# Local and global attention with a three-way max-out layer on one core: another literal order for the first third of the program

## The chip, the cores and the metric

The kernel runs on one core of one Trainium2 chip. The metric is device time in microseconds (us): a lower number is better. Five engines take part: PE (matrix products; PEld is its weight load), DVE (vector), ACT (scalar and activation), POOL (GpSimd) and SP, which here only issues DMA transfers.

## The reference

Batch 8, 8 heads, 576 positions, 64 per head. Attention is computed twice and added: once on q, k, v averaged over groups of four positions (144 of them), once on all positions but only within a band of three to either side. The sum, seen as 4608 tokens of 512 numbers, goes through a layer of three products whose maximum is taken, and a last product.

```python
out_d = sm_attn(q_d, k_d, v_d)                  # pooled by 4: 144 positions
out_up = np.repeat(out_d, factor, axis=2)
mask = np.abs(pos[:, None] - pos[None, :]) < factor
scores = np.where(mask, scale * np.matmul(q, k.transpose(0, 1, 3, 2)), -1000000000.0)
...
x = (out_up + out_local) as (4608, 512)
h = np.maximum(np.maximum(x @ w1, x @ w2), x @ w3)   # 512 -> 768
out = h @ w_out                                       # 768 -> 512
```

## The kernel before

**Tiling.** The eight batches are eight blocks j of 576 tokens, each cut into two halves n = 2j and 2j + 1. A half's pooled attention has scores (`ps`), a maximum taken negative (`nm`), an exponential on ACT, a sum whose reciprocal is `rd`, the scaled weights `pd`, `pdt`, `ptail`, their transposes on PE (`pt`, `ptt`), and the product with the pooled values (`vd` and `vs`, made from `hv` and `th`). For the first two blocks (n = 0 to 3, the dense ones) the band is done with matrix products as well: scores into a bank, maximum `mxb`, exponential, sum `zb`, and a multiplication by the reciprocal, all in one large tile whose traced name is `prod` (program name `early`). Other blocks do the band on DVE, POOL and ACT with elementwise products (`prod`, `pv`, `sums`). The max-out layer splits its numbers into a high and a low part: `xhi`, `xlo` for the tokens (made from `t` = `x` + `od`, the sum of both attentions) and `whi`, `wlo` for the weights (made from bf16 pieces `hh`, `wo`, `pv` and an f16 piece `hqk`). Three products (hi*hi, hi*lo, lo*hi) of 128x512 are added in a PSUM bank `pm`; the second product is `pm<-wo_0r,hh_0r`.

**Buffers.** PSUM has four banks `pm`, three `pa` and one `pq`. An operation that opens a bank waits until all readers of its previous use are done.

**What sets the order.** Every operation is recorded first, with a number (0 to 5409), its needs and the engines that may do it. A literal list, `TABLE` (lines 79 to 267), is then read word by word by `follow`: `546P` is operation 546 on PE, `145-146A` two operations on ACT; D is DVE, G is POOL, S is SP. `3F` stands for three fill products on PE (128x448, bf16, from a zeroed `prod`) whose results nobody reads; `warm` makes them. Within an engine the list's order is the order of the instructions, and its letters decide the engine. `take` also keeps a clock of estimated times from `price`, and by it chooses among the free buffers. `emit` then issues all instructions from one line, so that every instruction of the trace bears L765 (L764 in the changed kernel, whose file is one line shorter).

**Places that the text below speaks of.** Operation 546 is the first big product of the layer (block 0, `pm<-xhi_0r,whi_0r`); it needs 293 and 296 (`t<-x,od`, the attention's sum) and their casts 294, 297 (`xhi_0r<-t`) on ACT. Operation 104 (128x384) and 103 (128x256) are the last two multiplications of the dense band by the reciprocals (`prod<-prod,zb`) of half 1; their results are transposed on PE. 243 is the pooled attention's last product of half 1 (`pa<-pt,vd`). 361 and 362 are the corresponding multiplications of half 2, transposed by 375 to 378; 586 (`hh_0r<-pm,hh_0r`) is the end of the first max-out, and 628 the first product that opens its bank again.

Of the kernel before, what the change touches and what calls it, by code (L numbers as in the profile page):

```python
# [88 lines left out]
273S 559-562P 548P 347P 587P 549P 573-574P 303A 281A 299D 300A 289D 267D 274D 301D 304D 349P 550P 575P 563-564P 576-577P 565P 551P 578P 566-567P 579P
552P 568-569P 553-557P 580-582P 570P 583P 271A 343D 272D 290D 311A 282D 275D 312D 558A 247A 291A 276A 571D 584D 585A 335S 414S 345S 344S 415G 277G  # L90
374G 350P 387P 588-591P 613P 592P 600-602P 593-594P 614-618P 603-606P 619P 595-598P 607-608P 355-356D 351-352D 357A 353A 358D 354D 359-362D 1F
375-378P 609-610P 320S 449S 450G 283S 321A 313A 586D 380P 611P 628P 305S 346S 330S 451S 315S 887-888S 284A 285D 286A 306D 322D 287G 325S 381D 379A
599A 292G 416G 612D 307D 316A 317D 326D 331A 388P 382-383P 366-367S 323A 308A 324D 365D 371D 641P 629P 654P 642P 655P 630P 620-622P 631-637P 643-644P
638P 623P 639P 318A 640A 389P 624P 669P 309G 452G 645-648P 670-671P 649P 372D 327D 336A 332D 314D 337D 453D 368D 625D 417S 896S 496S 369-370S 461S
521S 386S 516S 459-460D 672P 650-652P 656-659P 673P 390P 660P 674P 661-665P 675-680P 395-396D 391-392D 653D 328A 512A 385A 418G 329G 319G 889A 338A
339G 373G 397A 398D 393A 681A 333A 506S 526S 895S 464S 498S 394D 419D 399-400D 402D 401D 682-689P 695P 408P 403-406P 690-692P 696P 693P 409A 407A
410-411P 697-706P 666D 667A 626A 513D 507-508D 522D 517A 384A 523D 668D 518D 694D 527-528D 627D 413A 509A 514A 412A 515G 519A 723P 420-421P 423D 422D
424D 524A 425-426A 529A 427-428A 890D 520G 710P 724-725P 736P 726-728P 737P 729-730P 738-740P 510G 741P 731P 711P 742-743P 712-713P 732P 714-715P
744-745P 716-717P 746P 718-721P 733P 536S 530D 497D 429-430A 431-432D 436D 438D 707D 433A 708A 434A 437D 439D 709D 537A 499G 525G 500G 462-463G 722A
440P 747P 442P 734P 435D 538D 735D 764P 468P 441P 751P 531S 465G 897A 532A 443-445P 765P 792P 752-757P 541S 448A 447A 446A 454P 758-762P 766-768P 926S  # L100
903S 908S 904S 533D 542D 748D 543D 534A 544A 749A 891D 750D 898D 471D 457-458A 455-456A 467P 769-771P 777P 535G 778-781P 466G 909G 1019S 1006S 927G
910G 1020G 928G 1021G 872G 875G 334G 900S 916S 970S 917G 901G 763A 905A 469-470D 899D 782-784P 793-794P 812P 785P 772P 813P 795P 814P 773-774P 786P
815P 796-797P 787P 798P 775P 799-802P 816-820P 803P 821-822P 788P 472A 539A 473A 906D 960S 1007S 912S 911S 474-477A 478-479D 485D 484A 545D 480A 486D
873A 902G 540G 968G 918G 874G 929S 892S 1500S 930G 489-492P 804P 823P 483D 776D 481-482D 789D 852P 487-488P 853P 824-825P 495A 494A 493A 790A 805P
501P 826P 854P 907D 913A 791D 827P 1128P 806P 828P 807-809P 1129P 829P 876A 502A 505A 503-504A 914-915D 1008A 830A 810A 893-894G 1501G 881G 978G 878G
931G 932P 935D 933-934D 919D 1502D 920-921D 936D 879A 880D 882A 937A 922A 938-939A 1009D 1014S 1016A 940A 923-924D 1010D 1035S 1484S 1015S 811S 1022S
1048S 831S 1485G 883G 1049G 925G 976G 877G 1017D 1030S 1508S 1023S 1036G 965G 1037G 972G 974G 1050G 1509G 1045S 1027S 966G 1510G 967G 1028G 855P
832-833P 1125P 856-857P 834-839P 858P 840-845P 859-866P 846P 1126P 1130P 1134P 847-849P 867P 1127P 1131P 868-869P 961A 850A 1018D 1166P 1132-1133P
1137-1139P 1143-1145P 870A 1151P 1135-1136P 1140-1142P 1146P 1152P 1147-1148P 1153P 1024A 975A 1025D 1149A 941A 942-943D 971A 1032A 945A 963-964A
1179P 1167-1168P 1154-1158P 1150D 1026D 1192P 1159-1162P 1169-1171P 1180P 1193-1194P 1172-1173P 1195P 1181P 1174P 1196-1199P 1175P 1200-1201P  # L110
1176-1177P 1202P 1182-1184P 1203P 1163D 948D 977G 1029G 973G 1164A 962A 1031S 1033D 990S 1479-1480S 1011S 950A 1178A 1481A 1165D 1220-1222P 1207P
1223P 1208P 1185-1188P 1209P 1189-1190P 1046G 979G 992A 995A 944A 991G 993G 1486G 994G 953P 1210P 1224-1226P 954-955P 1227-1228P 1211-1212P 1229P
1213-1217P 1034D 1038-1039D 1040G 1041A 1521S 1218P 980S 1230P 1614S 1487S 969D 1047G 1012G 988G 1013G 998G 996A 984A 982A 997A 851S 1089S 1488S 1606S
985G 981G 1000G 1522G 999G 1615G 947D 1482D 949D 986A 1191D 1204D 951P 946D 1483D 1042D 952P 956P 1219A 958A 1233-1237P 959D 1205A 957A 987A 983A
1206D 1274P 1231P 1232D 1043D 1044G 1238-1242P 1001P 1261-1262P 1243-1244P 1275P 1489A 1002A 1004-1005A 1003A 1248-1250P 1051P 1276-1278P 1251-1254P
1263P 1255-1256P 1279-1280P 1264-1265P 1257-1259P 1266-1269P 989D 1490D 1245D 1491D 1523G 1607G 1097G 1079S 1492S 1495S 1503S 1496S 1090A 1093G 1091A
1080A 1246A 1247D 1053D 1497A 1095A 1260A 1054D 1052D 1498D 1289P 1302P 1290-1292P 1303P 1293-1294P 1304P 1270-1271P 1295P 1272P 1296-1299P 1273D
1300P 1281P 1315P 1305P 1316P 1282-1283P 1317P 1284P 1499D 1081A 1085A 1055-1056A 1083A 1505A 1057A 1301A 1330P 1285P 1058-1060A 1061-1062D 1286D
1331-1332P 1306-1308P 1318P 1309P 1319-1321P 1333-1334P 1322P 1310-1311P 1335-1336P 1312-1313P 1323-1326P 1086G 1608G 1087G 1493-1494G 1096G 1084G
1094G 1082G 1598S 1518S 1599G 1519G 1092G 1098G 1520G 1632S 1633G 1616G 1504S 1099S 1609S 1109S 2042S 1103A 1287A 1506D 1288D 1067D 1064A 1069D 1066D  # L120
# [311 lines left out]
class Recorder:  # L432
# [104 lines left out]
    def price(self, eng, method, args, kw):  # L537

        out = kw["out"] if "out" in kw else args[0]
        n = elems(out)  # L540
# [4 lines left out]
        if eng == "PE":  # L545
# [3 lines left out]
            if args[1].dtype == F32R:  # L549
                return 226.7, False  # L550
# [1211 lines left out]
```

## Time and profile before

| | |
|---|---|
| device time, median of 3 runs | 684.52 us (684.20 to 684.93) |
| the profiled execution | 684.14 us; span of its trace 682.3 us |
| mean granted clock of PE | 0.999 |
| PE busy | 673.0 us, 99% |
| DVE / ACT / POOL busy | 616.1 / 403.5 / 392.9 us (90% / 59% / 58%) |

The span is the stretch from the first to the last instruction; 1.84 us of the profiled time lie around it. Busy times are sums over an engine's instructions; the share is of the span.

### The profile page before, as it was taken

How to read it: one execution, taken by the hardware profiler on the slowest of the kernel's cores; microseconds unless marked ns; L12 is line 12 of the kernel's file. 1: busy time of each engine (PE TensorE's matmuls, PEld its weight loads, DVE VectorE, ACT ScalarE, POOL GpSimd, SP SyncE). 2: the span in 40 equal slices, each digit the busy share in tenths (PEclk: the TensorE clock that was granted, in tenths of full speed). 3: DMA queues.
4: the chain of work that ended last, by engine and by line, in shares of the span. 5: the costliest groups of instructions: out<-in, count | busy, mean ns of one | idle time of the engine just before them, and what ended most of it. 6: DMA issues, size and time to landing. Idle time of an engine off the chain costs nothing.

```text
span 682.3 us, 12571 instructions
## 1 busy us (share of the span) xinstructions
PE 673.0 (99%) x4279; PEld 541.4 (79%) x4279; DVE 616.1 (90%) x846; ACT 403.5 (59%) x1366; POOL 392.9 (58%) x602
## 2 busy tenths in 40 slices
PE   7999999999999999999999999999999999999997
PEld 4678777878787788778877887788878888888886
DVE  7998999998999999999999999999998898999620
ACT  5955665788668457838675766457675654434121
POOL 3336377999989675939684977558356313332000
PEclk9999999999999999999999999999999999999999
DMA  9887475645455654435464535333430010000012
GB/s 317 298 294 264 166 224 174 202 153 182 145 180 164 207 182 155 152 126 175 146 190 138 160 124 159 106 107 97 144 97 19 1 61 1 1 0 1 0 62 62
DMA packets 50178, 92.79 MB, mean 136 GB/s; under 512 B 5540, under 2 KB 19426, under 8 KB 50114
## 3 DMA queue, kind: packets, MB, share of 16 engines
q1 hardware_dynamic: 50114, 91.99, 41.8%
q8 instruction: 33, 0.54, 0.3%
q14 instruction: 31, 0.25, 0.1%
HBM read 82.53 MB, written 9.44 MB: 135 GB/s over the span
## 4 chain that ended last, share of the span: by engine, by line
PE 96%; DVE 2%; DMA 1%; SPq 0%; issue 0%; ACT 0%; DVEq 0%
PE pm L765 80%; PE pa L765 14%; PE pq L765 2%; DMA whi<-in_kt_dense_dram 1%; DVE prod L765 1%; DVE zb L765 0%; DVE nm L765 0%; SPq L765 0%; DVE mxb L765 0%; DVE hh L765 0%; DVE t L765 0%; DVE wo L765 0%; DVE hqk L765 0%; DVE x L765 0%; DVE pd L765 0%
## 5 line engine op out<-in xcount | busy, mean ns | idle before, releaser
L765 PE MATMUL pm<-xhi_0r,wlo_0r 128*128 128x512 f32 x540 | 209.2, 393 | 0.0
L765 PE MATMUL pm<-xhi_0r,whi_0r 128*128 128x512 f32 x540 | 208.9, 394 | 0.0
L765 PE MATMUL pm<-xlo_0r,whi_0r 128*128 128x512 f32 x540 | 208.8, 394 | 0.0
L765 ACT ACTIVATE pv<-v,sums 128x64 f32<-128x64 f32 x564 | 148.5, 410 | 27.7 <-DVE x L765 12.1
L765 POOL TENSOR_TENSOR pv<-v,sums 128x256 f32<-128x256 f32 x237 | 143.0, 701 | 7.9 <-DVE x L765 5.8
L765 PE MATMUL pm<-wo_0r,hh_0r 128*128 128x512 f32 x576 | 142.1, 394 | 0.0
L765 PEld LDWEIGHTS pm<-wo_0r,hh_0r 128*128 128x128 f32 x576 | 106.4, 188 | 22.1 <-issue 0.7
L765 PEld LDWEIGHTS pm<-xlo_0r,whi_0r 128*128 128x128 f32 x540 | 101.4, 188 | 22.0 <-issue 1.6
L765 PEld LDWEIGHTS pm<-xhi_0r,whi_0r 128*128 128x128 f32 x540 | 101.4, 188 | 21.2 <-issue 1.2
L765 PEld LDWEIGHTS pm<-xhi_0r,wlo_0r 128*128 128x128 f32 x540 | 101.5, 188 | 21.1 <-issue 0.4
L765 DVE TENSOR_TENSOR prod<-k,pq 128x1792 f32<-128x1792 f32 x56 | 112.5, 2008 | 0.5
L765 DVE TENSOR_REDUCE sums<-prod 128x28 f32<-128x1792 f32 x56 | 112.1, 2002 | 0.3
L765 DVE TENSOR_REDUCE x<-pv 128x256 f32<-128x1792 f32 x40 | 79.8, 2009 | 0.8 <-POOL pv L765 0.8
L765 ACT COPY y<-pm 128x512 f32<-128x512 f32 (+1 forms) x50 | 28.7, 580 | 46.6 <-PE pm L765 38.4
L765 POOL TENSOR_TENSOR pv<-pv 128x768 f32<-128x768 f32 (+1 forms) x32 | 49.6, 1550 | 2.7 <-ACT pv L765 1.0
L765 POOL TENSOR_TENSOR x<-whi_0r,wlo_0r 128x512 f32<-128x512 f32 x16 | 22.9, 1445 | 47.4 <-DVE x L765 32.3
L765 ACT CAST hh_0r<-pm 128x512 fp32r<-128x512 f32 x47 | 27.6, 590 | 35.6 <-DVE pm L765 35.5
L765 ACT COPY t<-pm 128x512 f32<-128x512 f32 x42 | 24.6, 587 | 18.1 <-PE pm L765 17.7
L765 DVE TENSOR_TENSOR t<-pm,t 128x512 f32<-128x512 f32 x43 | 29.4, 684 | 6.0 <-PE pm L765 5.6
L765 ACT COPY pq<-q 128x256 f32<-128x256 f32 x56 | 22.2, 396 | 20.6 <-DVE prod L765 18.9
L765 DVE TENSOR_TENSOR pm<-pm,t 128x512 f32<-128x512 f32 x44 | 30.5, 693 | 4.1 <-PE pm L765 3.5
L765 DVE TENSOR_TENSOR hh_0r<-pm,hh_0r 128x512 fp32r<-128x512 f32 x47 | 32.1, 684 | 1.6 <-ACT hh_0r L765 1.4
(383 smaller groups left out, 1045.9 us busy)
## 6 DMA issues: line engine op xcount, KB each, us to landing
k<-in_k_dram SPq DMA_DIRECT2D x55, 320.0 KB
v<-in_v_dram SPq DMA_DIRECT2D x54, 320.0 KB
out_dram<-y SPq DMA_DIRECT2D x35, 256.0 KB
q<-in_q_dram SPq DMA_DIRECT2D x56, 128.0 KB
hqk<-in_kt_pool_dram SPq DMA_DIRECT2D x24, 256.0 KB
hqk<-in_qt_pool_dram SPq DMA_DIRECT2D x24, 256.0 KB
wo<-in_w_in_dram SPq DMA_DIRECT2D x8, 511.8 KB
hh<-in_w_in_dram SPq DMA_DIRECT2D x6, 511.8 KB
```

The costliest lines, as they stand in the source:

```text
L765: getattr(self.engines[o.eng], method)(*map(real, args), **{k: real(x) for k, x in kw.items()})
```

## The change

The list is another one from its 89th entry to about its 1980th of some 5443; the first 88 entries and the last 3463 are the same. As an engine sees it, the first 18 operations of PE, 29 of DVE, 23 of ACT, 6 of POOL and 23 of SP are unchanged, and so are the last 1980, 505, 464, 342 and 173. 122 operations go to another engine (DVE has 846 operations before and 856 now, ACT 795 and 799, POOL 563 and 549); there are 33 fills before and 32 now. The other edit is in `price`: the estimate for a big product is written as a formula, (512 + 32) / 2.4 = 226.7, which is the constant that stood there. The diff, with the list cut to one line of each:

```diff
 TABLE = """
 6S 11D 8D 2D 4D 18D 3D 9S 5D 0-1D 10S 340D 884-885D 7A 13-14S 126S 12S 129S 24-25P 167S 44P 21D 45P 169S 22D 1F 26P 19-20S 62D 42S 46P 27D 16S 127G
...
-188P 572P 348P 231P 229P 232-233P 547P 295G 230P 234P 187A 189A 1F 190P 269A 236-237A 235A 182A 266A 243P 245-246A 244A 191D 270D 262D 279A 302D 280D
...
             if args[1].dtype == F32R:
-                return 226.7, False
+                return (n + 32) / 2.4, False
```

What stands where now is seen in the order of the engines' instructions. On DVE, around the last multiplications of the dense band of half 1 (`prod<-prod,zb` with `zb_252`), before:

```order
L765 TENSOR_SCALAR zb_252<-zb_252 128x10
L765 TENSOR_TENSOR vs_538<-th_217 128x64
L765 RECIPROCAL zb_252<-zb_252 128x10
L765 TENSOR_TENSOR t_541<-x_376,od_461 128x512
L765 TENSOR_TENSOR hv_242<-v_168 128x256
L765 TENSOR_TENSOR t_544<-x_483,od_461 128x512
L765 TENSOR_TENSOR prod_119<-prod_119,zb_252 128x384
L765 TENSOR_TENSOR prod_119<-prod_119,zb_252 128x256
L765 TENSOR_SCALAR rd_335<-pa_238 128x5
```

and now, at the same place:

```order
L764 TENSOR_SCALAR zb_252<-zb_252 128x10
L764 RECIPROCAL zb_252<-zb_252 128x10
L764 TENSOR_TENSOR prod_119<-prod_119,zb_252 128x256
L764 TENSOR_TENSOR vd_514<-hv_242 128x256
L764 TENSOR_TENSOR prod_119<-prod_119,zb_252 128x384
L764 TENSOR_TENSOR t_517<-x_472,od_480 128x512
L764 TENSOR_TENSOR t_519<-x_386,od_480 128x512
L764 TENSOR_SCALAR rd_328<-pa_171 128x5
```

The two sums `t<-x,od` and the preparations `vs` and `hv` stood ahead of the two multiplications and are now behind them or gone from this engine; `vd`, which POOL made, is now on DVE between the two.

On PE, around the first big product (`xhi_0r,whi_0r`), a fill being a weight load and a 128x448 product of `prod_119`, before:

```order
L765 MATMUL pm_166<-prod_119 128x448
L765 MATMUL pq_431<-y_329,pv_257 64x58 x16
L765 MATMUL pq_431<-prod_119,pv_257 64x48 x2
L765 MATMUL pm_162<-ident_152,prod_119 128x128 x4
L765 MATMUL pm_156<-xhi_0r,whi_0r 128x512
L765 MATMUL pm_158<-ident_152,prod_119 128x128
L765 MATMUL pm_166<-xhi_0r,whi_0r 128x512
L765 LDWEIGHTS prod_119
L765 MATMUL pa_171<-prod_119 128x320
L765 MATMUL pa_230<-ident_152,pd_340 128x128
L765 MATMUL pa_238<-ident_152,pdt_343 128x128
```

and now:

```order
L764 MATMUL pm_156<-ident_152,prod_119 128x128
L764 LDWEIGHTS prod_119
L764 MATMUL pm_162<-prod_119 128x448
L764 MATMUL pm_166<-ident_152,prod_119 128x128
L764 MATMUL pq_451<-y_322,pv_257 64x58 x16
L764 MATMUL pq_451<-prod_119,pv_257 64x48 x2
L764 LDWEIGHTS prod_119
L764 MATMUL pm_158<-prod_119 128x448
L764 LDWEIGHTS prod_119
L764 MATMUL pm_162<-prod_119 128x448
L764 MATMUL pm_156<-ident_152,prod_119 128x128
L764 MATMUL pm_158<-xhi_0r,whi_0r 128x512
```

Before, the four transposes of operations 183 to 186 follow the band's products with `pv_257` in one run, and the fifth (188) comes behind the first big product. Now 183, 184 and 185 come earlier with fills between them (the row at the top is 185), then a fill, 188, the band's products, two fills and 186, and all five stand ahead of the first big product.

On PE, at the pooled weights of half 2 (`pdt`, `pd`, `ptail` transposed with `ident_152`), in the trace of before some 57 us behind the first big product, before:

```order
L765 MATMUL pm_162<-xhi_0r,wlo_0r 128x512
L765 MATMUL pa_171<-ident_152,pdt_343 128x128
L765 MATMUL pm_156<-xlo_0r,whi_0r 128x512
L765 MATMUL pa_238<-ident_152,pd_340 128x128
L765 MATMUL pm_162<-xlo_0r,whi_0r 128x512
L765 MATMUL pm_166<-xhi_0r,whi_0r 128x512
L765 MATMUL pa_230<-qkT_288 32x144 x4
L765 MATMUL pa_171<-ident_152,ptail_0_125 128x128
L765 MATMUL pm_158<-xhi_0r,whi_0r 128x512
L765 MATMUL pa_238<-ident_152,pd_340 128x128 x3
L765 MATMUL pm_166<-xhi_0r,wlo_0r 128x512
```

and now:

```order
L764 MATMUL pm_162<-xlo_0r,whi_0r 128x512
L764 MATMUL pm_156<-xlo_0r,whi_0r 128x512
L764 MATMUL pa_238<-ident_152,pd_368 128x128
L764 MATMUL pa_171<-ident_152,pdt_332 128x128
L764 MATMUL pa_171<-ident_152,ptail_0_125 128x128
L764 MATMUL pa_238<-ident_152,pd_368 128x128 x3
L764 MATMUL pm_162<-xhi_0r,whi_0r 128x512
```

The six transposes stood in four places between big products, and are now one run. Over the whole changed stretch the runs of transposes that have a big product on either side become fewer in this way: 28 before, 15 now.

## Rows read from the trace of the kernel before

**Rows 1.** The page: busy time by engine, and the chain that ended last.

```profile
PE 673.0 (99%) x4279; PEld 541.4 (79%) x4279; DVE 616.1 (90%) x846; ACT 403.5 (59%) x1366; POOL 392.9 (58%) x602
...
PE 96%; DVE 2%; DMA 1%; SPq 0%; issue 0%; ACT 0%; DVEq 0%
```

**Rows 2.** Waits of PE over the whole span: us in total, times, longest.

```profile
PE pm L765 <- DMA prod<-in_band_dram: 3.3, 1, 3.3
PE pm L765 <- DMA whi<-in_kt_dense_dram: 1.4, 2, 1.2
PE pm L765 <- DVE prod L765: 0.7, 3, 0.3
```

**Rows 3.** Busy time by stretch (start:end, length, engines, clock, DMA share, GB/s).

```profile
12.00:31.00 19.00, 18.28 (x272) 12.15 (x269) 18.39 (x55) 16.84 (x84) 7.04 (x11) 1.00 0.92 342
31.00:52.00 21.00, 21.00 (x293) 16.21 (x292) 20.54 (x42) 13.71 (x30) 5.79 (x6) 1.00 0.80 280
52.00:232.00 180.00, 180.00 (x1385) 143.11 (x1384) 168.17 (x221) 121.63 (x414) 146.88 (x216) 1.00 0.58 188
```

**Rows 4.** Timeline of PE around the first big product (start, us, instruction).

```profile
25.42 1.12 PE L765 MATMUL pm<-prod 128*128 128x448 bf16 x5
...
30.65 0.48 PE L765 MATMUL pm<-xhi_0r,whi_0r 128*128 128x512 f32 x1
...
33.94 0.71 PE L765 MATMUL pa<-pt,vd 128*64 128x144 f32 x8
```

**Rows 5.** Timeline of DVE, the multiplications of the dense band of half 1.

```profile
26.14 0.89 DVE L765 TENSOR_TENSOR prod<-prod,zb 128x256 f32<-128x256 f32 x2
...
27.29 0.63 DVE L765 TENSOR_TENSOR t<-x,od 128x512 f32<-128x512 f32 x1
27.83 0.42 DVE L765 TENSOR_TENSOR hv<-v 128x256 f32<-128x256 f32 x1
28.17 0.68 DVE L765 TENSOR_TENSOR t<-x,od 128x512 f32<-128x512 f32 x1
28.77 1.42 DVE L765 TENSOR_TENSOR prod<-prod,zb 128x384 f32<-128x384 f32 x2
```

**Rows 6.** Timeline of POOL and of ACT there, and the page's group of small ACT products.

```profile
28.33 1.11 POOL L765 TENSOR_TENSOR vd<-hv 128x256 f32<-128x256 f32 x1 [4.58 <-DVE hv L765]
...
29.00 0.14 ACT L765 ACTIVATION_READ_ACCUMULATOR pa<-pa,nm 128x1 f32 x1
29.05 1.14 ACT L765 CAST xhi_0r<-t 128x512 fp32r<-128x512 f32 x2
...
L765 ACT ACTIVATE pv<-v,sums 128x64 f32<-128x64 f32 x564 | 148.5, 410 | 27.7 <-DVE x L765 12.1
```

**Rows 7.** Timeline of PE: five transposes in one run, then two taken apart.

```profile
71.57 0.39 PE L765 MATMUL pm<-xhi_0r,whi_0r 128*128 128x512 f32 x1
71.80 0.71 PE L765 MATMUL pa<-ident,prod 128*128 128x128 f32 x5
72.26 0.48 PE L765 MATMUL pm<-xlo_0r,whi_0r 128*128 128x512 f32 x1
72.58 0.39 PE L765 MATMUL pm<-xhi_0r,whi_0r 128*128 128x512 f32 x1
...
87.45 0.39 PE L765 MATMUL pm<-xhi_0r,wlo_0r 128*128 128x512 f32 x1
87.68 0.27 PE L765 MATMUL pa<-ident,pdt 128*128 128x128 f32 x1
87.70 0.48 PE L765 MATMUL pm<-xlo_0r,whi_0r 128*128 128x512 f32 x1
88.02 0.27 PE L765 MATMUL pa<-ident,pd 128*128 128x128 f32 x1
...
88.36 0.40 PE L765 MATMUL pm<-xhi_0r,whi_0r 128*128 128x512 f32 x1
```

**Rows 8.** Timeline of DVE and of PE near 50 us, half 2's multiplications and transposes.

```profile
49.12 0.90 DVE L765 TENSOR_TENSOR prod<-prod,zb 128x256 f32<-128x256 f32 x2
49.93 0.69 DVE L765 TENSOR_TENSOR hh_0r<-pm,hh_0r 128x512 fp32r<-128x512 f32 x1
...
51.54 0.60 PE L765 MATMUL pa<-ident,prod 128*128 128x128 f32 x4
```

More of the change, by code (lines that the diff above doesn't have):

```diff
@@ L89 @@
[L89 to L120, printed above, removed]
@@ new lines @@
+1094A 1273D 1274P 1300P 1093A 1056-1059A 1498-1499D 1518S 1503S 1505A 1301A 1333-1341P 1342A 1090A 1302P 1085-1086G 1082G 1080G 1083G 1523G 1084G
+1081G 1088G 1593S 1508S 1509G 1614S 1095G 1510G 1519G 1097G 1504S 1099S 1275-1279P 1060A 1506D 1109S 1098G 1303P 1280P 1343P 1281P 1344-1345P
+1282-1285P 1061-1062D 1066D 1068D 1507D 1286D 1511D 1069D 1595A 1067A 1106A 1315P 1304-1312P 1316-1323P 1313P 1314D 1064D 1458-1459P 1346P 1324-1326P
+1100A 1104A 1287A 1288D 1347P 1072-1074P 1460-1461P 1348P 1356-1357P 1107G 1116G 1112G 1117G 1101G 1115G 1111G 1103A 1110A 1113A 1327D 1512D
@@ new lines @@
+1472P 1465P 1604D 1389A 1554A 1568-1569A 1611A 1605D 1455D 1567A 1456A 1473-1474P 1466P 1475P 1398P 1414-1417P 1432P 1399P 1418-1420P 1433-1436P
+1421-1423P 1476D 1561D 1612D 1400-1401P 1467-1468P 1424-1427P 1457D 1469D 1402-1403P 1428P 1429A 1617S 1619A 1477A 1437P 1711P 1404-1405P 1712P 1406P
+1438-1439P 1714P 1407P 1715-1716P 1720P 1408P 1618S 1390S 1636G 1560G 1565G 1570G 1563G 1600G 1637G 2058S 1632S 2042S 1582S 1616G 1564G 1571G 1572S
+1613D 1478D 1585A 1470A 1471D 1409A 1587A 1589G 1588G 1586G 1584G 1573G 2043G 1575G 1590G 1633G 1574G 1576A 1583A 1579A 1620-1621D 1625-1627D
@@ new lines @@
+1440-1443P 1713P 1444-1447P 1717P 1752P 1448P 1753-1755P 2046S 2037S 1410S 2045S 2066S 2076S 2038S 1680S 1580G 1592G 1718P 1756P 1524P 1721P 1449A
+1577A 1719P 1723P 1757-1759P 1765-1767P 1724P 1768P 1722P 1769P 1760P 1725P 1578A 1628A 1527D 1526D 1629D 1525D 1528D 1761P 1729-1731P 1735A
+1762-1763P 1529-1530A 2039A 1531-1532A 1764A 1533A 1581D 1630D 1591D 1726-1728P 1737-1738P 1732-1733P 1739P 1734P 1770-1776P 1736D 1777D 1740-1744P
+1806-1807P 1745-1747P 1793P 1748P 2059-2060G 2044G 2067G 1688G 1631G 1670S 1675G 2050S 1634G 1671G 2051-2052G 1681G 1683G 1674G 2196S 2204S 2077G
@@ new lines @@
+2666S 1872D 2192S 1884-1885P 2065D 1886P 1873A 1888-1889P 1887A 1890-1891P 2649G 2185A 2082P 2199S 1874D 2656S 2186D 1892P 2634G 1893P 2650G 1894P
+2083A 1895P 2084A 2641G 2085A 1896P 2086A 1897P 2187D 2200S 1898P 2227G 1899P 2778S 1901P 2667G 2193A 1902-1903P 2642G 2207S 1904-1905P 2657G 2669S
+1906-1907P 1900D 2087P 2668G 2088-2089P 2786S 2090P 2069D 1908P 2070D 1909P 2194D 1910P 2658G 1911-1912P 2071G 1916-1921P 1913D 2072A 2779G 2208S
+1922-1923P 2091D 1924P 1914A 1925P 2670G 2794S 1926P 2073D 2201A 1927P 1915D 2812S 1929-1930P 1928A 2627S 2074D 1931P 2195D 1932-1934P 2075G
```

78 lines of the change are left out of this document (47 added, 31 removed).

## The prediction

> **What bounds the kernel now.** I read the page first. PE is busy 673.0 us of the span of 682.3, and the chain that ended last runs through PE for 96% of it [rows 1]. The reader is to see that no other engine's share matters by itself; an order can change the time only by letting PE start or go on at another time, or by giving PE the same operations in a dearer or cheaper row.
>
> So the second view is what PE waits for. There are three rows, 5.4 us in all, two of them for first loads, and 0.7 us for DVE's `prod` [rows 2]. They all lie in the start. Between 31 and 232 us PE is busy for 201.0 of 201.0 us, at full clock [rows 3]. Where an engine never waits, a better order behind it has nothing to gain. In the start, from 12 to 31 us, PE is busy 18.28 of 19.00 us, DVE 18.39 and ACT 16.84 [rows 3]: here the softmax of the dense halves runs on DVE and ACT, and much of PE's busy time is fills, which nobody needs. Five of them take 1.12 us, some 0.2 us each once the last one's tail of about 0.2 is taken off [rows 4]. The first big product starts at 30.65 [rows 4]; from there on the time is a queue of PE work of fixed length, so each microsecond by which that start moves is one of the span, unless a wait comes later.
>
> The median of the runs is 684.52, the profiled execution took 684.14, 0.38 less. I make the sum against the profiled one (span 682.3 and 1.84 around it) and forecast the median by adding 0.38. A measurement of this kernel tells a change from none at about 0.2%, that is 1.37 us.
>
> **The change part by part.**
>
> *The formula in the price.* It gives 226.7 for 512 columns, as before, and no instruction comes from it: 0.
>
> *The start, up to the first big product.* The last multiplications of half 1's dense band, 104 and 103, feed the last transposes ahead of it. Ahead of 104 on DVE two sums, `hv` and `vs` are gone. By start-to-start steps the first sum costs 0.54, `hv` 0.34, the second sum 0.60 [rows 5], with 0.14 for `vs` 1.6 us. `vd` comes in; it is a product of 256 columns like `hv`, 0.34. That leaves -1.3. Besides, 104 and 103 took 1.42 us in before, while POOL's `vd` ran from 28.33 to 29.44 [rows 6]; their twins, a 256 and a 384 wide one too, took 0.89 without it [rows 5]. With `vd` on DVE itself the 0.53 go. [...] Further up the list other small pieces come to DVE and leave it; by steps of the same pieces in before they add about 0.5. Sum: DVE is through with 104 about 1.3 us earlier, near 28.5.
>
> That is not what the first big product gets, for three reasons. The two sums now stand behind 104, and each costs 0.54 to 0.60, so they end near 29.1 and 29.7 instead of 27.9 and 28.9. ACT has six small multiplications more (POOL did them before): at 148.5 us for 564 such products, 0.26 each, 1.6 us [rows 6]. In before its casts of the sums began at 29.05, right behind the last exponential (29.00) [rows 6]; now the exponentials end some 0.4 later and the casts follow. And PE has its own list: two fills between single transposes, the band's products (`y`,`pv`) behind 188, and the fifth transpose ahead of the first big product instead of behind it. Following these through I get 31.0 to 31.4 for the first big product, 0.3 to 0.8 late, but with work done that came behind it before. The fair mark is 243, the pooled attention's last product of half 1, since the same operations stand ahead of it in both lists but for the fills (31 before, 30 now). It started at 33.94 [rows 4]; I get 33.8 to 34.3. I take -0.1.
>
> Bounds: all that PE can gain from 12 us on is its idle time, 19.00 - 18.28 = 0.72, and the one fill, 0.2: -0.9. In the other direction ACT's 1.6 us come half through: +0.8.
>
> *The order of PE after that.* The same operations, but transposes in longer runs (15 runs between big products instead of 28). In before, five in one run: from the big product at 71.57 over the transposes to the second one behind them at 72.58 are 1.01 us with two products in it; at 0.227 a product (by the steps of 0.23 between products that stand together) 0.56 remain, 0.111 for each transpose. Two taken apart: from 87.45 to 88.36 are 0.91 us with three products, so 0.23 for two, 0.115 each [rows 7]. The reader must not be taken in by the 0.02 between the lone transpose at 87.68 and its product at 87.70: that product then takes until 88.02, 0.32, where others take 0.23. So a run costs the same as the transposes apart, and the 13 fewer runs bring 13 x 0.004, less than 0.1. I take 0, and -0.2 to +0.2 for all orders of the other products.
>
> *Half 2 near 50 us.* This is the thinnest place of the new list. From the start of 104 (28.77) to that of 361 (49.12) DVE had 42 operations and 20.35 us [rows 5, 8], and hardly a pause: 20.54 of 21.00 busy [rows 3]. In the new list five of these are gone and ten come in between (the two sums, two `hv`, five sums of 512 columns or the like, 362): 1.9 us out, 5.0 in, by their steps, -0.5 for the multiplications' contention. With the start of 104 0.8 us earlier 361 ends near 50.0 to 50.8 instead of 49.55. PE wants it for the transposes at 51.54 [rows 8] in before, and near 50.7 in the new order, which has less PE work ahead of them. Just behind, 586, that freed its bank at 50.62 [rows 8], is now near 50.6 to 51.4, and 628 wants the bank near 51.2. So the slack of some 2 us becomes 0 to 0.7. Behind 361 on DVE stands 586, so both are late together and PE is made to wait once: I take 0.2, between 0 and 1.
>
> *The rest, 52 to 232 us.* DVE is busy 168.17 of 180, ACT 121.63, POOL 146.88, PE all of it [rows 3]. The new list gives POOL 14 operations less and DVE 10 more, most of them in the start; by the running sums of work in both lists everything that PE needs is 5 us or more ahead. I take 0; if that cover were gone, a stall would be as long as the lateness.
>
> Sum: -0.1 + 0 + 0.2 + 0 = +0.1, so 684.24 for a profiled run like that of before, and a median of 684.6.
>
> **The rivals.**
>
> *Faster: the start gains all it can.* For it speaks that DVE is through with 104 1.3 us earlier. Against it that PE's own list in the start is full; what it can give is 0.9 [rows 3, 4], with 0.2 from the order: 684.52 - 1.1 = 683.4. To be faster by over 1.37 us it would need a gain ahead of 12 us as well, where first loads decide and these are the same. Chance of being faster by over 0.2%: 0.12.
>
> *Slower: DVE is late for half 2.* One mechanism: the 3 us more work between 104 and 361 are not covered by the earlier start of 104. From a lateness of about 0.7 us at 361 PE waits, and then one for one. If 104 ends where it did before (29.85), 361 ends at 51.4 plus pauses of up to 0.7, PE waits 0.7 to 1.4 at the transposes, and 586 holds the bank for as much again at most; with a late start of 0.8, 2 to 3 us: 686.5 to 687.5. Chance 0.2.
>
> *Slower: runs of transposes are dear.* If a lone transpose cost only the 0.02 between its start and the product's, against 0.11 in a run, 13 fewer gaps would cost 13 x 0.09 = 1.2 us: 685.8 with the 0.1 above. Against it speak the 0.32 of the product behind [rows 7]. [...] Chance 0.05, mostly still within 0.2%.
>
> **How the numbers follow.** No measurable change has 0.63: the terms all lie within 1 us of each other's cancelling, and the largest possible gain is below the bound. Faster by over 0.2% 0.12, for a start that I have understood wrongly. Slower by over 0.2% 0.25: 0.2 for half 2 and 0.05 for the other stalls of a new order and for the transposes. The range goes from the faster rival's 683.4 up to 686.5, where the late half 2 begins to leave it; 0.1 stays out on either side.
>
> **What would show it.** Right: PE's waits are 5 to 6 us with nothing in it beyond 52 us; 104 ends near 28.5 on DVE; 243 starts between 33.2 and 34.8; between 52 and 232 us PE is busy throughout; a run of transposes costs 0.11 each. Half 2 shows as a wait for DVE's `prod` or `hh` near 50 us of up to 1 us. Wrong would be a wait of PE of more than 1 us beyond 31 us, for DVE or ACT (late rival), a first big product before 30.0 (faster rival), or a stretch of PE without waits that takes longer than before.

## The result, and the profile after

The changed kernel is slower: the median of 13 runs is 689.32 us (687.50 to 696.23) against 685.36 (684.19 to 686.67) for the kernel before in 13 runs beside them, a ratio of 1.0074 [1.0049, 1.0098]. The forecast was 684.6 in 683.4 to 686.5, so the time lies outside the range. The profiled execution took 696.23 us (span 694.5), 12.1 more than that of before. It is the slowest of the 13: ten took 687.50 to 690.24 us at a mean granted clock of 0.999 or more, three took 693.15 to 696.23 at 0.990 to 0.993.

The page: busy time by engine, and the chain that ended last (these answer to [rows 1]).

```profile
PE 678.9 (98%) x4278; PEld 546.4 (79%) x4278; DVE 618.2 (89%) x856; ACT 407.3 (59%) x1380; POOL 384.8 (55%) x590
...
PE 84%; DMA 1%; POOL 0%; ACT 0%; SPq 0%; issue 0%
```

The waits of PE over the whole span (us in total, times, longest), which answer to [rows 2].

```profile
PE pa L764 <- DVE prod L764: 3.6, 1, 3.6
PE pm L764 <- DMA prod<-in_band_dram: 3.2, 1, 3.2
PE pm L764 <- DMA whi<-in_kt_dense_dram: 1.5, 1, 1.5
PE pm L764 <- DVE prod L764: 1.4, 2, 1.0
```

The two first loads are as before. The first row is new, and the last has doubled. Where they lie is seen in the busy time by stretch (columns as in [rows 3], 52 to 232 us cut finer).

```profile
12.00:31.00 19.00, 16.28 (x225) 10.41 (x224) 17.19 (x50) 16.99 (x87) 7.15 (x10) 1.00 1.04 391
31.00:52.00 21.00, 21.00 (x323) 16.16 (x321) 20.20 (x41) 12.18 (x27) 4.15 (x3) 1.00 0.66 218
52.00:58.00 6.00, 2.38 (x12) 1.75 (x11) 4.43 (x8) 3.13 (x6) 2.37 (x2) 0.84 0.58 225
58.00:70.00 12.00, 12.00 (x182) 10.02 (x181) 5.33 (x10) 4.59 (x9) 1.75 (x2) 0.51 0.54 160
70.00:232.00 162.00, 161.56 (x1152) 128.33 (x1151) 150.21 (x204) 111.23 (x383) 121.98 (x181) 1.00 0.54 171
```

Three things are to be seen. In the start PE is busy for 2.0 us less than before in the same 19. Near 55 us it stands still, for 3.62 us. Behind that the granted clock is 0.51 for 12 us, though PE then never pauses (12.00 of 12.00 us busy). From 70 us on PE pauses for 0.44 us only.

PE's timeline at the two places:

```profile
33.33 0.48 PE L764 MATMUL pm<-xhi_0r,whi_0r 128*128 128x512 f32 x1
...
36.20 0.71 PE L764 MATMUL pa<-pt,vd 128*64 128x144 f32 x8
...
57.44 1.30 PE L764 MATMUL pa<-ident,prod 128*128 128x128 f32 x5 [3.62 <-DVE prod L764]
```

The first big product starts at 33.33 instead of 30.65 and 243, the mark that the prediction chose, at 36.20 instead of 33.94 [rows 4]: 2.26 late. The transposes of half 2 (375 to 378) wait 3.62 us for DVE's multiplications 361 and 362.

From 243 to the first of the last 1980 operations of PE, which are the same in both lists, are 207.35 us, and 197.59 in before: 9.76 more. Of them 4.06 are waits that the trace shows. Another execution of the same kernel (e1_again, below) had no stretch at a low clock; there the way was 201.22 with 2.95 of waits. Without the waits the two differ by 203.29 - 198.27 = 5.0 us: that is what the stretch at 0.51 cost in this execution. So the profiled 12.1 are 2.3 for the start, 4.1 for waits, 5.0 for the clock and 0.7 that stay; for e1_again, 5.67 above before, they are 2.0 + 2.95 + 0.7. In e1_again these 0.7 stand at the operations that wait (375, 442, 454, 723) and right behind them, 0.07 to 0.3 at each against the same steps of e2_act284_late. They may be parts of those waits that the profile shows short; no run shows it.

### The profile page after: what moved, and what is told of

The parts are those of the page before. It is cut to its first block, busy times and chain, and to the rows that moved or that the text cites. A ratio compares the mean times of both kernels' runs of the same rounds, so it can differ in the third digit from the quotient of the medians.

```text
span 694.5 us, 12572 instructions
## 1 busy us (share of the span) xinstructions
PE 678.9 (98%) x4278; PEld 546.4 (79%) x4278; DVE 618.2 (89%) x856; ACT 407.3 (59%) x1380; POOL 384.8 (55%) x590
## 4 chain that ended last, share of the span: by engine, by line
PE 84%; DMA 1%; POOL 0%; ACT 0%; SPq 0%; issue 0%
PE pm L764 71%; PE pa L764 11%; PE pq L764 2%; DMA q<-in_q_dram 1%; POOL wlo_0r L764 0%; SPq L764 0%; ACT whi_0r L764 0%; ACT pq L764 0%; ACT y L764 0%; DMA wo<-in_w_in_dram 0%; ACT pt L764 0%
## 5 line engine op out<-in xcount | busy, mean ns | idle before, releaser
L764 DVE TENSOR_REDUCE x<-pv 128x256 f32<-128x1792 f32 x39 | 77.8, 2005 | 0.7 <-POOL pv L764 0.6
L764 POOL TENSOR_TENSOR pv<-pv 128x768 f32<-128x768 f32 (+1 forms) x34 | 53.0, 1560 | 6.4 <-ACT pv L764 4.9
```

Of the source, the lines that this page charges most:

```text
L764: getattr(self.engines[o.eng], method)(*map(real, args), **{k: real(x) for k, x in kw.items()})
```

## The experiments

Each ratio, with its 95% interval, is against the kernel before in runs beside it on the same chip (it is not the quotient of the two medians). "243" is the start of that operation, "way" the time from it to PE's common last part, "idle" what of the way the trace shows as waits.

| | ratio [95%] | median us | 243 | way | idle |
|---|---|---|---|---|---|
| before (profiled) | 1 | 685.36 | 33.94 | 197.59 | 0.00 |
| after | 1.0074 [1.0049, 1.0098] | 689.32 | 36.20 | 207.35 | 4.06 |
| e1_again | 1.0060 [1.0047, 1.0074] | 689.86 | 35.92 | 201.22 | 2.95 |
| e2_act284_late | 1.0058 [1.0043, 1.0073] | 689.61 | 35.68 | 198.86 | 1.11 |
| e3_start_before | 1.0039 [1.0018, 1.0059] | 687.22 | 33.30 | 200.78 | 2.26 |
| e4_start_after | 1.0042 [1.0026, 1.0058] | 688.32 | 37.08 | 198.48 | 0.55 |
| e5_dve_order | 1.0073 [1.0048, 1.0098] | 689.05 | 35.68 | 199.49 | 2.04 |
| e6_wlo_on_dve | 1.0097 [1.0076, 1.0119] | 691.16 | 34.87 | 201.94 | 2.79 |
| e7_both_and_284 | 1.0034 [1.0024, 1.0044] | 687.46 | 33.92 | 201.24 | 1.98 |
| e8_before_284_early | 1.0032 [1.0020, 1.0045] | 687.05 | 34.03 | 199.29 | 1.42 |
| e9_loads_half3 | 1.0116 [1.0103, 1.0129] | 692.97 | 34.55 | 204.71 | 4.48 |
| e10_fills_at_389 | 1.0045 [1.0031, 1.0060] | 687.52 | 33.99 | 200.47 | 0.67 |
| e11_fills_at_375 | 1.0104 [1.0090, 1.0118] | 691.75 | 35.55 | 202.60 | 2.27 |
| e12_loads_and_415 | 1.0068 [1.0053, 1.0082] | 689.99 | 34.44 | 202.18 | 2.62 |
| e13_415_behind | 1.0053 [1.0034, 1.0072] | 689.52 | 33.70 | 203.32 | 3.72 |
| e14_414_415_before | 1.0046 [1.0032, 1.0059] | 687.74 | 34.97 | 201.28 | 2.32 |
| e15_414_and_loads | 1.0036 [1.0023, 1.0050] | 687.10 | 33.76 | 201.08 | 2.25 |
| e16_before_to_454 | 0.9998 [0.9987, 1.0008] | 685.07 | 34.10 | 198.44 | 0.61 |
| e17_897_behind | 1.0027 [1.0016, 1.0038] | 687.26 | 34.06 | 200.29 | 1.86 |

**Theories.** Mine, after the two traces: the time is lost in two places, each by an engine that stands waiting with the wanted operation queued behind: DVE in the start, ACT near 50 us; the low clock is a consequence. Rivals: the prediction's own (DVE simply has too much work ahead of 361), PE's new order by itself, and a clock that fell for another reason.

**The changed kernel again.** No edit.

> The changed kernel once more, for a second trace of it. In its first trace TensorE lost time at two places: the start (the pooled attention's last product of half 1 began at 36.20 us instead of 33.94, 2.3 us late) and one wait of 3.6 us at 53.8 us, after which the granted clock fell to about half up to some 69 us. Theory (two places): typical runs have both, with a shorter wait and no fall of the clock: ratio 1.005 to 1.007; the start again 2.0 to 2.5 us late, the wait 1 to 4 us. Rival (the time is spread over the whole changed stretch, by dearer rows of transposes): the same ratio, but the start and the wait explain less than half of it, and the stretch from 70 to 232 us is over 2 us longer than before.

It is 0.6% slower with the clock at 1.00 throughout, so this loss needs no low clock. Its waits of PE beyond 31 us (first fence), and ACT and PE near 50 us (second):

```profile
PE pa L764 <- DVE prod L764: 1.5, 1, 1.5
PE pa L764 <- ACT pt L764: 0.8, 1, 0.8
PE pm L764 <- ACT whi_0r L764: 0.5, 1, 0.5
PE pa L764 <- ACT pd L764: 0.2, 1, 0.2
```

```profile
49.46 0.77 ACT L764 CAST hqk<-wo 128x512 f16<-128x512 bf16 x1 [3.32 <-DMA wo<-in_w_in_dram]
...
54.98 0.74 PE L764 MATMUL pa<-ident,prod 128*128 128x128 f32 x5 [1.48 <-DVE prod L764]
```

The cast is operation 284. It had to wait 3.32 us for load 283, and half 2's exponentials 357 and 353 stand behind it. But in this execution that wait costs PE nothing: the exponentials end at 50.93, and DVE, which its own list keeps busy without a pause from 28 us on, comes to their sums at 50.94. What makes DVE late at 375 is seen in its own rows, and in POOL's:

```profile
50.94 0.87 DVE L764 TENSOR_REDUCE zb<-prod 128x10 f32<-128x320 f32 x2
51.73 0.68 DVE L764 SCALAR_TENSOR_TENSOR wo<-wo,hqk 128x512 uint32<-128x512 uint32 x1
...
52.84 1.99 DVE L764 TENSOR_TENSOR prod<-prod,zb 128x384 f32<-128x384 f32 x2
```

```profile
53.18 1.37 POOL L764 TENSOR_TENSOR wlo_0r<-wo,whi_0r 128x512 fp32r<-128x512 f32 x1 [5.23 <-ACT whi_0r L764]
```

With 284 early, 285 (`wo<-wo,hqk`) stands on DVE ahead of the multiplications, and 287, the subtraction on POOL that makes the low part of this weight piece, runs beside them. The two multiplications 362 and 361 took 0.90 us together in before [rows 8] and take 1.99 here; 361 alone takes 1.51.

**284 behind the exponentials**, with its load where it was; 285 and 286 go behind the multiplications and 586. All else of the changed list stays.

```diff
-283S 284A 357A 353A 312D 358D 354D 585A 285D 359-360D 362D 361D 286A 313A 586D 375-377P
+283S 357A 353A 312D 358D 354D 585A 284A 359-360D 362D 361D 313A 586D 285D 286A 375-377P
```

> The changed list with operations 284 (ACT, reads the weight piece rawin_2_1 that arrived at about 52 us), 285 and 286 put behind the exponentials 357, 353, the cast 585 and the max 586. Theory (a late load ahead of the exponentials on ACT): the wait at 53.8 us goes down to below 0.7 us, the start's 2.3 us stay: ratio 1.0025 to 1.0040. Rival (DVE alone is late for half 2, as the prediction's slower rival has it, and ACT's place is no matter): the wait stays at 2 to 4 us and the ratio at 1.005 to 1.007.

The wait at 375 is gone in the trace. DVE's rows there:

```profile
50.70 0.87 DVE L764 TENSOR_REDUCE zb<-prod 128x10 f32<-128x320 f32 x2
...
52.13 0.89 DVE L764 TENSOR_TENSOR prod<-prod,zb 128x384 f32<-128x384 f32 x2
```

The sums come 0.24 us earlier than in e1_again, and so does 243: the exponentials gave DVE nothing. The multiplications end 1.81 us earlier: 0.24 from the start, 0.47 since 285 is not ahead of them, 1.10 since POOL's 287 begins at 54.99. So the early place of 284 makes the wait, by way of 285 and 287. In the profiled execution of the changed kernel the late load comes on top: there DVE waits 2.09 us for ACT's exponentials, and 1.48 + 2.09 is the wait of 3.62 but for 0.05. No run moves 287 by itself.

The profiled execution took 687.22, but the other five took 689.39 to 690.08, no less than e1_again. In the trace PE waits 0.69 and 0.39 further on, at 389 and 390, for two loads of half 3's scores. Against e1_again the trace gains 2.6 us, the median (689.61 against 689.86) nothing that can be measured. What the five slower executions waited for has no trace and stays open.

**The two parts apart.** In e3 the list is before's as far as 243 and the changed order behind; in e4 the other way round.

```diff
 e3, before's list up to 243, then the changed list's rest
-... 243P 245-246A 244A 191D 270D 262D 279A ...
+... 243P 449S 451S 315S 273S 191A ...
 e4, the changed list up to 243, then before's rest
-... 451S 310S 315S 273S 243P 191A ...
+... 451S 310S 315S 273S 243P 511S 886S 298D 364D ...
```

> The list of before up to operation 243 (the pooled attention's last product of half 1), and from there on the remaining operations in the order and on the engines of the changed list. Theory (two places): the start's 2.3 us are gone (243 starts at 33.9 plus or minus 0.3); the late load stays ahead of the exponentials, so the wait near 52 us stays at 1 to 4 us: ratio 1.002 to 1.006. Rival (everything comes from the late start, the wait too): ratio 0.999 to 1.001.

> The changed list up to operation 243, and from there on the remaining operations in the order and on the engines of before. Theory (two places): the start is 2.3 us late, and nothing more: ratio 1.0025 to 1.0045, no wait of TensorE over 0.7 us beyond 40 us. Rival (rows of transposes of the later list are what costs): ratio 0.999 to 1.002.

Each part alone costs about 0.4%. In e3 243 starts at 33.30, no later than before, and ACT's cast still waits 3.43 us, the multiplications take 1.99 and PE waits 1.50 at the transposes: half 2 needs no late start for its wait. In e4 the way is 0.9 longer than before and nearly all is the start's 3.1; of these 0.74 is a wait of PE at 34.35 that the changed kernel does not have.

**DVE's order in the start.** In the changed list 211, the maximum over half 1's pooled scores, stands ahead of 255 and of the band's reciprocals and multiplications; DVE waits there for PE. Its timeline, of the changed kernel:

```profile
25.91 0.46 DVE L764 TENSOR_REDUCE nm<-pa 128x2 f32<-128x288 f32 x1 [0.91 <-PE pa L764]
26.28 0.68 DVE L764 SCALAR_TENSOR_TENSOR hh<-hh,hqk 128x512 uint32<-128x512 uint32 x1
...
27.55 0.90 DVE L764 TENSOR_TENSOR prod<-prod,zb 128x256 f32<-128x256 f32 x2
28.81 1.34 DVE L764 TENSOR_TENSOR prod<-prod,zb 128x256 f32<-128x256 f32 x1
30.07 0.54 DVE L764 TENSOR_TENSOR vd<-hv 128x256 f32<-128x256 f32 x1
30.53 0.55 DVE L764 TENSOR_TENSOR prod<-prod,zb 128x384 f32<-128x384 f32 x1
31.00 1.28 DVE L764 TENSOR_TENSOR t<-x,od 128x512 f32<-128x512 f32 x2
```

And POOL's, at the same time:

```profile
28.57 1.29 POOL L764 TENSOR_TENSOR wlo_0r<-hh,whi_0r 128x512 fp32r<-128x512 f32 x1 [4.29 <-ACT whi_0r L764]
```

103 takes 1.34 us beside POOL's 257, 104 takes 0.55 beside none, and ends at 31.08 instead of near 28.5. e5 puts 211 and 213 behind 255 and 122; e6 puts 257 on DVE behind the multiplications; e7 does both, and e2's edit too.

```diff
 e5
-254D 211D 255D 213D 122D 214D 123-125D
+254-255D 122D 211D 213D 123D 214D 124-125D
 e6
-288S 201G 257G 202G 228D 224D 363D
+288S 201G 202G 228D 224D 257D 363D
```

> The changed list with six entries of DVE in another order: 255 (0.7 us on a weight piece) and 122 (reciprocal chain of the dense band) ahead of 211, the maximum that waits for TensorE's pooled scores, as in before; everything else as in the changed list. Theory (the start is late since DVE waits 0.9 us at 211 with the band's reciprocals and multiplications queued behind it): the wait at 211 shrinks below 0.3 us, 103 begins 0.7 to 1.2 us earlier, operation 243 0.5 to 1.2 us earlier than the 35.9 to 36.2 of the changed list: ratio 1.0035 to 1.0055. Rival (TensorE's own order with its fills sets the start): 243 moves by less than 0.3 us, ratio 1.0055 to 1.007.

> The changed list with one operation on another engine: 257, the low part of a weight piece, on DVE behind 224 instead of on POOL, where it ran beside 103. Theory (contention of the two engines): 103 takes 0.4 us instead of 1.33, the transpose behind it (183) comes 0.7 to 1.0 us earlier, 243 0.3 to 0.9 us earlier: ratio 1.0045 to 1.006, the wait near 54 us no shorter, since DVE has 0.6 us more. Rival (103 is long for another reason): 103 stays above 1 us and 243 where it was.

> The two edits on the start together (255 and 122 ahead of 211; 257 on DVE) and 284, 285, 286 behind the exponentials and the max 586. Theory (start plus late load): 243 begins within 0.7 us of before's 33.94, no wait of TensorE of over 1 us beyond 40 us: ratio 1.000 to 1.003. Rival (a further cost in the changed list that neither place shows): ratio above 1.003.

e5 takes away the wait at 211, but 103 still meets POOL: it begins earlier, takes 1.55 us and ends 0.28 behind POOL's 257, as in the changed kernel. 243 stands at 35.68, where e2 has it without that edit: by itself it gives nothing that shows. In e6 103 takes 0.42 (DVE's timeline, below) while the wait at 211 is as in the changed kernel, and 243 comes at 34.87; the four traces with the changed start (after, e1, e2, e11) have it at 35.55 to 36.20. With both, in e7, 104 ends at 28.67 and 243 starts at 33.92, where before has it. The contention is shown (103: 1.34 us with 257 on POOL, 0.42 with it on DVE). 211's part rests on the one trace of e6: others with e7's start (e9, e10, e12, e13) have 243 at 33.70 to 34.55, 0.3 to 1.2 ahead of e6.

```profile
25.49 0.46 DVE L764 TENSOR_REDUCE nm<-pa 128x2 f32<-128x288 f32 x1 [0.90 <-PE pa L764]
...
28.39 0.42 DVE L764 TENSOR_TENSOR prod<-prod,zb 128x256 f32<-128x256 f32 x1
...
29.07 0.55 DVE L764 TENSOR_TENSOR prod<-prod,zb 128x384 f32<-128x384 f32 x1
```

The median of e6 is none the better for it: its wait at 375 is 1.92 (DVE waits 0.40 for ACT's exponentials there), and the clock 0.93 between 52 and 75 us. In e7, with start and half 2 mended, 0.34% remain; PE waits at half 3's scores (389).

```profile
62.73 0.89 PE L764 MATMUL pa<-wlo 64*26 64x32 f32 x80 [1.70 <-DVE qkT L764]
```

**The late load in the kernel before.** Loads 320, 449, 283 and the cast 284 go ahead of the exponentials there, as in the changed list.

```diff
-351-352D 357A 353A 358D 354D
+351-352D 320S 449S 283S 284A 285D 357A 353A 358D 354D
```

> The list of before with one thing of the changed list: the ACT cast 284 and DVE's 285, which need the weight piece rawin_2_1, stand ahead of the exponentials 357, 353 and the sums 358, 354 of half 2 (the loads 320, 449, 283 stand earlier in the list for it, in the same order on their queue). Theory (head of the line): ACT waits 2 to 4 us for the load, TensorE 1 to 3 us for the transposes 375 to 378 near 52 us: ratio 1.0015 to 1.0045, with a start as in before. Rival (only the changed list's crowded loads make it late): TensorE's wait below 0.5 us, ratio 0.999 to 1.001.

This alone makes the kernel before 0.32% slower, as the theory had it, but not in its way. ACT waits 0.90 at 284, and the multiplications begin at 50.20 instead of 49.12, with 285 ahead of them; yet the transposes start at 51.61, 0.07 later than in before [rows 8] and without a wait. PE's wait of 1.12 comes 3 us later, at products that want a copy by DVE (`prod<-pa`, 54.18 instead of 52.75). Ahead of that copy one DVE operation takes 1.78 us, in before 0.68: POOL's subtractions run beside it, from 50.61 on instead of 52.02.

```profile
50.61 3.11 POOL L764 TENSOR_TENSOR wlo_0r<-wo,whi_0r 128x512 fp32r<-128x512 f32 x2 [2.35 <-ACT whi_0r L764]
52.48 1.78 DVE L764 SCALAR_TENSOR_TENSOR hh<-hh,hqk 128x512 uint32<-128x512 uint32 x1
54.52 0.24 PE L764 MATMUL pa<-y,wlo 32*64 32x26 f32 x2 [1.12 <-DVE prod L764]
```

Another 0.31 is a wait at 82.6 us for `hh_0r`.

**Half 3.** In the changed list SP issues the loads of half 3's scores (366, 367) and of `traw` (414) later, behind others, and DVE's 415 (`th<-traw`, which needs 414) stands ahead of 371, which PE's scores want. e9 (on e7) issues 366 and 367 earlier; e12 also has 414 earlier and 415 behind 371; e13 moves 415 alone.

```diff
 e9
-283S 511S 887S 330S 305S 386S 325S 496S 367S 366S
+283S 305S 330S 325S 366S 367S 496S 511S 887S 386S
 e12
+283S 305S 330S 511S 887S 325S 366S 367S 414S 496S 386S
 e12 and e13
-414S 415D ... 389P 371D 329D 309D
+414S ... 389P 371D 329D 309D 415D
```

> As e7, and besides another order of ten loads on SP's queue: behind 283 come 305, 330, 325, then 366 and 367 (half 3's q and k), and only then 496, 511, 887 and 386, which the changed list had put ahead of them. Theory (the rest of the changed list's loss is a third late load): TensorE's wait of 1.7 us at operation 389, the pooled-to-band scores of half 3 near 62 us, goes below 0.5 us, the granted clock stays at 1.00 behind it: ratio 0.999 to 1.0015. Rival (the loads take as long in this order too, or something else of the list costs): the wait stays above 1 us or the ratio above 1.002.

> As e7, and DVE's operation 415 (`th` of half 4's tail, which waits for the load 414) behind 309 instead of ahead of 371, and SP's loads behind 283 in the order 305, 330, 511, 887, 325, 366, 367, 414, 496, 386. Theory (all of the loss are waits for late loads ahead of others in an engine's line, and the late start): no wait of TensorE of over 0.5 us beyond 40 us, clock 1.00, 243 near 34: ratio 0.999 to 1.001. Rival (the changed list has a further cost): ratio 1.002 or more with no such wait.

> As e7, with one more edit: 415 behind 309 on DVE; the loads in the changed list's order. Theory (415 in DVE's line ahead of 371 and 309, waiting for load 414, is the third place): the wait at 389 shrinks by the 0.34 us and more that DVE stood at 415 and by 415's 0.85, to below 0.8 us: ratio 1.000 to 1.0025. Rival (the loads 366, 367 themselves are late): the wait at 389 stays at 1 us or more, ratio 1.0025 to 1.0045.

The medians of all three are above e7's (e13's interval overlaps with e7's), and each shows a wait in another place. In e9 414 is now the late one, and DVE stands at 415 for 3.92 us:

```profile
66.74 0.29 DVE L764 TENSOR_TENSOR th<-traw 128x128 f32<-128x128 f32 x1 [3.92 <-DMA traw<-in_qkt_tail_dram]
```

With it PE waits 4.3 us for `wlo_0r` at 670, and the clock is 0.57 between 67 and 75 us. In e13 415 runs late, so its buffer comes free late, and SP, which issues load 461 into it, stands there with half 3's loads 369 and 370 behind (the waits of SP's queue, and of PE, from 50 to 75 us):

```profile
SPq L764 <- DVE th L764: 3.2, 1, 3.2
```

```profile
PE pa L764 <- DMA wlo<-in_kt_dense_dram: 2.2, 1, 2.2
```

In e12 PE's wait of that name is 1.7.

**All of them in step.** e14 has 414 and 415 where before has them (on POOL, ahead of 243); e15 besides issues 366 and 367 ahead of 496, 335 and 386, and 369 and 370 ahead of 461; e17 besides moves 897 on ACT, which waits for a load of `q` at 96 us with 446 behind it, on which PE's 454 depends.

```diff
 e14
-315S 273S 243P
+315S 273S 414S 415G 243P
 e15
-461S 369-370S
+369-370S 461S
 e17
-466D 897A 754-762P 534A 446A 763A
+466D 754-762P 534A 446A 897A 763A
```

> As e7, and the load 414 and its reader 415 (`th` of the next half's tail) back where before has them: 414 behind 273 on SP's queue (some 36 us instead of 58), 415 on POOL then. In the changed list 414 came late, DVE stood at 415 for it, and the load 461, which takes over 415's buffer, blocked SP's queue ahead of 369 and 370. Theory (that chain is the third place): no wait of TensorE over 0.7 us at 389 or 390, ratio 1.000 to 1.002. Rival (366, 367, 369, 370 are late by themselves): a wait of 1 us or more at 389 or 390, ratio 1.003 to 1.006 as in e7 and e13.

> As e14, and half 3's loads 366 and 367 ahead of 496, 335 and 386 on SP's queue, and 461 behind 370, as before has them. Theory: all late loads are gone: 243 near 34, no wait of over 0.5 us beyond 40 us, clock 1.00: ratio 0.999 to 1.001. Rival (the changed list has a cost besides): ratio 1.002 or more.

> As e15, with ACT's operation 897 (a copy of q, which waits for its load) behind 446 instead of ahead of it; 446's result goes into 454, where TensorE waited 0.6 to 0.8 us near 96 us in e1 and e15. Theory (once more a reader of a late load ahead in an engine's line): that wait goes below 0.3 us; ratio 1.002 to 1.0035, 0 to 0.8 us less than e15. Rival (446 is late by itself): the wait at 454 stays at 0.5 us or more.

No single wait is over 0.9 us any more, but their sum (2.32, 2.25 and 1.86 us) is hardly below e7's 1.98, and no ratio is clear of e7's 1.0034. e17 is the lowest at 1.0027, with 454's wait gone and two others left beyond 31 us:

```profile
PE pm L764 <- ACT whi_0r L764: 0.9, 1, 0.9
PE pm L764 <- DVE wlo_0r L764: 0.7, 1, 0.7
```

**Before's list as far as 454**, some 95 us, and the changed order behind it.

```diff
-... 448A 447A 446A 454P (before's next words)
+... 448A 447A 446A 454P 533D 891D 334G 904S ...
```

> The list of before up to operation 454 (the pooled product of half 2, 95 us in before), and from there on the remaining operations in the order and on the engines of the changed list, to its end at some 231 us. Theory (all of the loss arises ahead of 98 us; the changed order of the later two thirds of the stretch, transposes in longer runs among them, is worth nothing): ratio 0.999 to 1.001, no wait of TensorE of over 0.7 us beyond 98 us. Rival (that part costs too): ratio 1.0015 or more.

0.9998 [0.9987, 1.0008], with waits of 0.4 and 0.2 left beyond 31 us: the changed order from there to about 230 us costs nothing that is measured, and all of the loss lies ahead of it. This kernel has the formula in the price too, so that is cleared as well.

**The clock.** e10 (on e7) puts 9 fills ahead of 389, where PE waits; e11 (on the changed list) 14 ahead of 375.

```diff
 e10
-336A 389P
+336A 9F 389P
 e11
-586D 375-377P
+586D 14F 375-377P
```

> As e7, with nine more fill products of TensorE (0.19 us each, 1.7 us) ahead of operation 389, where it waited for 1.7 us and the granted clock then stood at 0.56 to 0.59 from 64 to 68 us. Theory (a wait costs twice, once by itself and once by the clock behind it): 389 starts no later, the clock stays at 1.00, the stretch of products behind 389 takes 0.23 us each, ratio 1.0005 to 1.0025. Rival (the clock falls for another reason): it falls again between 62 and 70 us and the ratio stays at 1.003 or more.

> The changed list with fourteen more fills (2.7 us) ahead of the transposes 375, where it waited 1.5 us in one trace and 3.6 in another, the latter with the granted clock at 0.50 for some 13 us behind it. Theory (the runs of 693 us and more are those with the long wait and the fallen clock): no run above 692 us, clock 1.00 from 54 to 70 us; the median within 1 us of the 689.3 to 689.9 of the changed list, since fills stand in for the wait. Rival: runs above 692 us again, in 1 of 5.

In e10 the clock stays at 1.00, where e7 had 0.57 between 64 and 68 us:

```profile
61.12 1.86 PE L764 MATMUL pm<-prod 128*128 128x448 bf16 x9
```

(e10), and between 64 and 68 us of e7 and of e10:

```profile
64.00:68.00 4.00, 4.00 (x12) 3.10 (x11) 2.22 (x5) 2.50 (x4) 1.00 (x1) 0.57 0.66 171
```

```profile
64.00:68.00 4.00, 4.00 (x19) 3.25 (x19) 1.02 (x3) 1.68 (x3) 2.22 (x3) 1.00 0.73 201
```

Its median, 687.52, is that of e7, 687.46, above what the theory had. That says little of the clock: of e7's twelve executions only the profiled one has a mean clock below 0.999 (0.997), so the others had hardly anything to win back. Fills don't repair the wait itself. e11 missed: the fills need a bank themselves and waited 1.6 us for 586, with all behind them; it is dearer than the changed kernel, and one of its five executions took 693.70, as the rival had it.

## Why the prediction was wrong

**The start.** The prediction has "DVE is through with 104 about 1.3 us earlier, near 28.5" and takes -0.1 at 243. Measured are +1.6 to +2.3 in four traces (after, e1, e2, e11), beyond its bound of +0.8, and 104 ends at 31.08. This is the first failed step. It added up work along DVE's list and left out what DVE waits for: 211 needs PE's scores, and 0.91 us pass there with the whole band behind it. And it let POOL's contention vanish with `vd`, which is right for 104 (0.55), but 257 had gone to POOL in the same list, and 103 meets it (1.34 against 0.42). Without these two, in e7, the prediction's own figures come out: 104 ends at 28.67 and 243 starts at 33.92 (forecast 33.8 to 34.3). The prediction's own reading of the contention, 1.42 us beside POOL's `vd` against 0.89 without it [rows 5, 6], had to be held against every POOL instruction of the new list, not only against the one that left.

**The order of PE.** Taken as 0, and nothing measured speaks against it: in e2 PE has all of the changed order behind 243, and its way without shown waits is 197.75 against 197.59. The rival of dear transposes falls, and the formula in the price makes no instruction.

**Half 2.** The prediction looked at the right place ("the thinnest place of the new list") and took 0.2 us, from DVE's additional work. The wait was 1.48 to 3.62. The additional work itself was well sized: from the start of 104 to that of the multiplications DVE needs 22.59 us in e1_again, against 20.35 in before and some 22.95 by the prediction's terms. Two other steps failed. 104 was taken to be early and was late. And the multiplications were taken to be as long as in before, though POOL's 287 now runs beside them: that is 1.10 of the 1.48 us. It is the error of the start a second time, the contention with POOL (361: 1.51 us beside 287, 0.42 without it in e9) again not held against the new list. The wait stands with a start as early as before's (e3) and goes with 284 to 286 behind the exponentials (e2). e8 puts 284 and 285 ahead of them in the kernel before: there POOL's subtractions meet other DVE operations and PE waits elsewhere.

The late load makes the profiled execution worse. SP issues 283 at 45.99 instead of 43.15, right behind DVE's 282, the last reader of the buffer, which ends 2.8 us later than before. From there to the cast 6.3 us pass, in e1_again 3.8; why is open. ACT's timeline in the profiled execution of the changed kernel:

```profile
45.87 0.59 ACT L764 COPY t<-pm 128x512 f32<-128x512 f32 x1 [1.09 <-PE pm L764]
52.26 0.78 ACT L764 CAST hqk<-wo 128x512 f16<-128x512 bf16 x1 [5.80 <-DMA wo<-in_w_in_dram]
52.90 0.82 ACT L764 ACTIVATE prod<-prod 128x320 f32<-128x320 f32 x2
```

ACT does nothing for 5.80 us, though the first exponential behind the cast has had its numbers from DVE since 49.19: it stands behind the cast in ACT's list and begins at 52.90, the cast at 52.26.

**The rest.** The prediction has "everything that PE needs is 5 us or more ahead. I take 0". From about 95 us on this holds (e16). Between 62 and 96 us it failed by the same error: running sums of work show no engine that stands before a late load. There the waits are 1.70 in e7 and 1.61 in e17.

**The rival on the slow side** had the right sign and place, and DVE's work behind a late 104 is a part of what happened. Its price, 686.5 to 687.5, was too small: it had 104 at most 0.8 late (1.5 in e1_again) and nothing of POOL. The price of the low clock was in no term.

**What stays open.** Why e17 is still at 1.0027: the two waits left, 1.6 us, are at 670 and 723, and what makes `wlo_0r` and `whi_0r` late there was not followed further; another 0.8 us of its way is in no wait that the trace shows. What e2's untraced executions waited for. And what 287 costs by itself, since no run moved it alone. No mended version beat the kernel before.

## What to carry to other kernels

A new order has to be followed as queues, not as sums of work: for each instruction that needs a load or another engine, ask when that comes and what stands behind it on its engine, and the same of SP's queue, where here load 461 waited 3.2 us for the last reader of its buffer (e13). Here several loads had become late together, and moving one moved the wait to the next: e9 has no wait at 389, where e7 had 1.70 us, and 4.3 at 670. A DVE multiplication on the path like 103 and 361 is to be held against every POOL instruction that may run beside it, at every place of the new list: here it cost in the start (103: 1.34 us against 0.42) and in half 2 (361: 1.51 against 0.42).

## What was not expected of the hardware

One wait of PE cost more than its length: behind 3.62 us of waiting PE ran for 12 us at a granted clock of 0.51, busy all the time, and that cost 5.0 us more. Behind 1.70 (e7) came 4 us at 0.57; behind 1.48 (e1_again) the clock stayed at 1.00. A 256 wide DVE multiplication took 0.42 us alone (103 in e6 and e7) and 1.33 to 1.55 beside a 512 wide POOL subtraction (103 in after, e1 and e5, 361 in after). Its length went with the subtraction's end: in all seven cases of four traces (103 in after, e1 and e5, 361 in after, e1, e5 and e6) in which it begins while that subtraction runs, it ends 0.27 to 0.29 us behind the subtraction's end. 362, which in after begins 0.33 us ahead of POOL's 287, takes 0.56 there and 0.55 in before.
